# Wide exponents with the bias added by GpSimd, and low words of weights on ScalarE, in a Mamba-2 scan with an ELU layer

## The chip, the cores and the metric

The kernel runs on one core of a Trainium2 chip. The metric is the device time of one execution in microseconds (us); smaller is better. Five engines work from queues of their own, each strictly in its order: PE (TensorE, matrix products, with a separate weight load PEld), DVE (VectorE), ACT (ScalarE), POOL (GpSimd) and SP (SyncE, which here issues DMAs). PE writes to PSUM, a small memory that DVE and ACT read; the other tiles lie in SBUF.

## What is computed

The reference is a state-space scan (Mamba-2, in chunks) followed by a feed-forward layer with an ELU:

```python
# per batch b and head h, chunks c of 32 tokens (batch 4, heads 8, tokens 768, head_dim 32, state 16)
cum = np.cumsum(np.log(np.clip(a, 1e-6, 1.0)), axis=-1)        # within a chunk
L = np.exp(cum[:, :, :, None] - cum[:, :, None, :]) * causal   # "decay"
y_intra = einsum((C @ B.T) * L, x)
y_inter = einsum(C, state) * exp(cum)
state = decay_full * state + sum(B x * decay_from_j)
# then, on the 3072 tokens x 256 features
h = x @ w_in                                                   # 256 -> 2048
g = np.where(h > 0, h, np.exp(np.minimum(h, 0)) - 1)           # ELU
out = g @ w_out                                                # 2048 -> 256
```

The weights arrive as 64-bit floats. The kernel puts them together from their two 32-bit words itself.

## The kernel before

**Blocks.** The work is cut into twelve blocks `n` of 256 tokens (two halves `u` of 128; each half has two chunks `v` of 64 tokens, the chunk length that the kernel uses). Blocks two and three (`n` = 2 and 3) are those that the change touches.

**Decays.** For each block a tile `L` of 128 partitions x [8 heads, 2 halves, 64] is filled by a DMA that spreads the running sums along the partitions (`spread_cum`, L382). `decay_of(n, h)` (from L517) turns it into the decay of head `h` in place: two instructions on ACT (L521), each of 64 columns, take the exponent with a bias `ncum`, one column of [128, 1] for each half and head. After each fourth head, POOL sets what is not causal to zero with two `affine_select`s (L526), one for each chunk. `decay(n, q)` does heads 2q and 2q+1. `weigh(n, q)` (L550, DVE) then multiplies a PSUM tile of scores by two heads of `L`.

**Weight pieces.** There are 16 pieces of weights (0 to 7 are `w_in`, 8 to 15 `w_out`), each 128 x 512 numbers. For a piece `i`, `w_take` issues the absolute value of the high words on ACT (L196), the low words, and the signs on DVE (L223); `w_give` issues two DVE steps (L231, then L238) and the sum with the low words on POOL (L248). The low words are `x * 2**-51 + 2`. `w_low` can do them on DVE (L209) or on ACT (L205, with the bias from a column named `two`). Before the change, pieces 5 to 15 have them on DVE.

**The first layer, and the ELU.** `l1(n, i)` makes one product of the first layer, 8 matrix products (L666) into one PSUM tile, and appends it to a list `lag`. `elu()` takes the oldest: relu on ACT (L679), exponent on ACT (L686), and a combination on DVE (L688), which is the last reader of the PSUM tile. `l2(n, j)` adds to the second layer's sum (L826).

**PSUM.** Seven buffers hold all of these: products of `l1`, the four tiles of `scores` (L541), the state sums (`sums`, L571), the turned inputs (`turn`, L428, then L433 on ACT and L436 and L444 on DVE) and the four tiles of y (`across` L616, `inside` L634, copied out by ACT at L651). An eighth belongs to the second layer and some state sums. A product can only begin when a buffer has been read out.

**The order** is written out by hand: each engine's queue holds its instructions in the order in which the code issues them. Around the change there are two loops. The first has twelve steps `s`, each with one product `l1`; in its body stand, in this order, the decays of block two, `scores`, `sums` and the first two `weigh` of block two (step 7), a weight piece (`w_take`, `w_give`, in odd steps, pieces 5 to 10), `turn(2)` (step 5), the other `weigh` and `states(2)` (step 8), the first half of block three's decays (step 9), `across` and `inside` of block two (step 10), and at the end of the step the oldest `elu()` if more than one product waits:

```python
        if s < 8:
            decay_of(2, s)
        ...
        if s % 2 == 1 and todo < 11:
            w_take(todo, nc.vector)
            w_give(todo)
```

The second loop has eight steps `j`, with products of blocks two and three and pieces 11 to 15 (`j` = 0, 2, 3, 4, 5). Step 0 issues `turn(3)`, `w_give`, the waiting `elu()`s and then the second half of block three's decays; step 1 `scores(3)`, `sums(3)` and the four `weigh(3, q)`; step 2 `states(3)`; step 3 `inside(across(3), 3)`. Through `scan_ahead` it also takes the decays of blocks four and five, which the change does not touch, and from step 4 the preparation of a three-product form of the first layer (L735, L736, L754 to L771, L786) used for all later blocks, for which POOL subtracts parts of weights (L842).

Of the kernel before, what the change touches and what calls it, by code (L numbers as in the profile page):

```python
# [14 lines left out]
ALU = mybir.AluOpType  # L15
ACT = mybir.ActivationFunctionType

P = 128
Q = 64
# [13 lines left out]
def kernel(  # L33
# [27 lines left out]
    nc = tc.nc  # L61
    NB, NH, S, D = x.shape
    N = B.shape[-1]
    NG = S // BLK
# [27 lines left out]
    for k in range(4):  # L92
        (nc.scalar if k % 2 else nc.sync).dma_start(
            out=la0[BH * k:BH * (k + 1)],
            in_=a.rearrange("b h (c s) -> (b h) c s", s=P)[:, 0:2, :])
# [5 lines left out]
    st = {}  # L101

    def place(n):

        return 2 * (n // (2 * NG)) + n % 2, n // 2 % NG

    def rows_of(n):
        b, g = place(n)
        return slice(NG * NH * b + g, NG * NH * (b + 1), NG)
# [80 lines left out]
    def w_abs(i, cols=slice(None)):  # L190
        if i in (1, 2) or cols.start:
            w_abs_of[i, cols.start] = psum([P, 2, CW], "ps_mag").bitcast(U32)
        if i not in w_mag:
            w_mag[i] = (ffn.tile([P, 2, CW], U32, tag="tmp", name="mag", bufs=1) if i == 2 else
                        ffn.tile([P, 2, CW], U32, tag="g0", name="mag", bufs=12))
        nc.scalar.activation(  # L196
            w_abs_of.get((i, cols.start), w_mag[i])[:, :, cols].bitcast(F32),
            w_words(i)[1][:, :, cols].bitcast(F32), ACT.Abs)
# [4 lines left out]
    def w_low(i, eng, cols=slice(None)):  # L203
        if eng is nc.scalar:
            eng.activation(  # L205
                pieces[i][0][:, :, cols], w_words(i)[0][:, :, cols], ACT.Identity,
                scale=2.0 ** -51, bias=two)
        else:
            eng.tensor_scalar(  # L209
                out=pieces[i][0], in0=w_words(i)[0], scalar1=2.0 ** -51, scalar2=2.0,  # L210
                op0=ALU.mult, op1=ALU.add)
# [3 lines left out]
    def w_sign(i, cols=slice(None), eng=nc.vector):  # L215
        if i not in w_sgn:
            w_sgn[i] = ffn.tile([P, 2, CW], U32, tag="g1", name="sgn", bufs=12)
        if eng is nc.gpsimd:
            eng.tensor_scalar(
                out=w_sgn[i][:, :, cols], in0=w_words(i)[1][:, :, cols].bitcast(mybir.dt.int32),  # L220
                scalar1=0.0, scalar2=2.0 ** 31, op0=ALU.is_lt, op1=ALU.mult)
            return
        nc.vector.tensor_scalar(  # L223
            out=w_sgn[i][:, :, cols], in0=w_words(i)[1][:, :, cols], scalar1=0x80000000,
            scalar2=None, op0=ALU.bitwise_and)
# [53 lines left out]
    for v in range(2):  # L279
        nc.gpsimd.affine_select(  # L280
            out=low16[Q * v:Q * v + Q], in_=low16[Q * v:Q * v + Q], pattern=[[1, Q]],
            compare_op=ALU.is_ge, fill=-65536.0, base=0, channel_multiplier=-1)
# [4 lines left out]
        out=hmask, in_=hmask, pattern=[[-N, NH]], compare_op=ALU.is_ge, fill=0.0,  # L287
        base=0, channel_multiplier=1)
    nc.gpsimd.affine_select(
        out=hmask, in_=hmask, pattern=[[N, NH]], compare_op=ALU.is_ge, fill=0.0,  # L290
        base=N - 1, channel_multiplier=-1)
# [7 lines left out]
        out=minus, in0=ident, scalar1=-1.0, scalar2=None, op0=ALU.mult)  # L299


    heads = [first[:, 3, n].rearrange("p (h n) -> p h n", n=N) for n in range(2)]
# [57 lines left out]
    def turned(src, name, scale, eng):  # L360
        rows = src.shape[0]
        ps = psum([P, 2, rows], "ps_" + name)
        for u in range(2):
            nc.tensor.transpose(out=ps[:, u], in_=src[:, u], identity=ident[0:rows, 0:rows])
        t = const.tile([P, 2, rows], F32, name=name)
        if eng is nc.scalar:
            eng.copy(out=t, in_=ps)
        else:
            eng.tensor_scalar(out=t, in0=ps, scalar1=scale, scalar2=None, op0=ALU.mult)
        return t  # L370
# [142 lines left out]
    def decay(n, q):  # L513

        decay_of(n, 2 * q)
        decay_of(n, 2 * q + 1)

    def decay_of(n, h):
        L, row = st[n]["L"], rows_of(n).start + NG * h
        for u in range(2):  # L520
            nc.scalar.activation(  # L521
                L[:, h, u], L[:, h, u], ACT.Exp, bias=ncum[:, u, row:row + 1])
        if h % 4 == 3:
            for v in range(2):
                part = L[Q * v:Q * v + Q, h - 3:h + 1]
                nc.gpsimd.affine_select(  # L526
                    out=part, in_=part, pattern=[[0, 4], [0, 2], [1, Q]],
                    compare_op=ALU.is_ge, fill=0.0, base=0, channel_multiplier=-1)

# [15 lines left out]
    def weigh(n, q):  # L547
        s = st[n]
        M = att.tile([P, 2, 2, Q], F32, tag="M", name="M", bufs=8)
        nc.vector.tensor_tensor(  # L550
            out=M, in0=s["g"][q],
            in1=s["L"][:, 2 * q:2 * q + 2].rearrange("p k u i -> p u k i"), op=ALU.mult)
        s["M"].append(M)
# [104 lines left out]
    def l1(n, i, parts=1):  # L658

        ps = psum([P, 2, BLK], "ps_h")  # L660
        for j in range(2):
            m = 2 * i + j
            for part in range(parts):
                toks = slice(part * BLK // parts, (part + 1) * BLK // parts)
                for k in range(KC):
                    nc.tensor.matmul(  # L666
                        out=ps[:, j, toks], lhsT=w_in[i][:, k, j * P:(j + 1) * P],
                        rhs=yT[n // 2][:, k, n % 2].rearrange("p u i -> p (u i)")[:, toks],
                        start=(k == 0), stop=(k == KC - 1))
        lag.append((n, i, ps))  # L670
# [292 lines left out]
    def w_take(i, low):  # L963

        w_abs(i)
        w_low(i, low)
        w_sign(i)
# [15 lines left out]
    half = [slice(0, P), slice(P, 2 * P)]  # L983
# [97 lines left out]
    ncum = turned(F[:, 0], "ncum", -1.0, nc.vector)  # L1081
# [6 lines left out]
    todo = 5  # L1088
    for s, (n, i) in enumerate((
            (1, 0), (1, 1), (1, 2), (0, 4), (1, 3), (0, 5), (1, 4), (0, 6), (1, 5), (0, 7),  # L1090
            (1, 6), (1, 7))):
        l1(n, i, parts=2 if s < 2 else 1)
        if s < 8:
            decay_of(2, s)
        if s == 7:
            st[0] = kept
            scores(2)
            sums(2, 0, pool=p_o, tag="o", parts=(None, last))
            weigh(2, 0)
            weigh(2, 1)  # L1100
        if s % 2 == 1 and todo < 11:
            w_take(todo, nc.vector)
            w_give(todo)
            w_load(todo + 6)
            todo += 1
        if s in (1, 3):
            load_bc(3, us=(s // 2,))
        if s == 9:
            write_flat(0)
        if s == 4:  # L1110
            scaled(2, nc.gpsimd)
        if s == 5:
            turn(2)
            turn_exp(2)
        if s == 4:
            load_x(3)
            spread_exp(3)
        if s == 8:
            weigh(2, 2)
            weigh(2, 3)  # L1120
            states(0, last)
            st.pop(0)
            states(2)
        if s == 9:
            decay(3, 0)
            decay(3, 1)
        if s == 10:
            spread_cum(4)
            inside(across(2), 2)
        if len(lag) > 1:  # L1130
            elu()
# [38 lines left out]
    for j in range(2 * DIRECT):  # L1170
        n, i = 2 + j // DIRECT, j % DIRECT
        if j < 7:
            l2(0, j)
        piece = todo < len(pieces) and j != 1
        if j == 0:
            elu()
        if piece:
            w_take(todo, nc.vector)
        l1(n, i)
        if j == 7:  # L1180
            l2(0, j)
        if j == 0:
            scaled(3, nc.gpsimd)
            turn(3)
            elu()
            turn_exp(3)
        if piece:
            w_give(todo)
            todo += 1
        while lag:  # L1190
            elu()
        if j == 0:
            decay(3, 2)
            decay(3, 3)
        if j == 1:
            scores(3)
            sums(3)
            for q in range(4):
                weigh(3, q)
        if j == 2:  # L1200
            states(3)
        if j == 3:
            inside(across(3), 3)
        if j == 4:
            words_of_y(2)
        if j == 4:
            words_of_w(4)
        if j == 5:
            low_of_w(4)
        if j == 5:  # L1210
            both_of_y(2)
        scan_ahead(j)
        if j == 3:
            s_out[:] = weight_sums()
        if j == 6:
            differences(0, 4)
        if j == 7:
            words_of_w(5)
# [126 lines left out]
    n = NP - 2  # L1345
# [34 lines left out]
```

## Time and profile before

| | |
|---|---|
| median of 3 runs | 352.54 us (352.52 to 353.02) |
| span of the profiled execution, first to last instruction | 351.1 us |
| time of the profiled execution outside its span | not listed by itself; the median of the runs is 1.44 us above the span |
| TensorE clock granted | 1.000 |
| L521, exponents of 64 columns, all blocks | 160 instructions, 42.2 us, mean 337 ns |
| L526, masks on POOL | 40 instructions, 29.3 us, mean 733 ns |
| L209, low words on DVE | 11 instructions, 407 to 866 ns |
| L205, low words on ACT, 128x512 | 4 instructions, mean 753 ns |
| L248, sums of weight pieces on POOL, 128x512 | 15 instructions, mean 1276 to 1320 ns |
| L679 and L686, relu and exponent of the ELU, 128x512 | 24 each, mean 590 and 631 ns |

How to read it: the profile is that of one execution. A line such as L521 is a line of the kernel. A row of the timeline has the start in us, the duration in us, the engine, the line, the operation, the tile written and the tiles read, the shapes, and a count if instructions of one kind follow on each other; in brackets stand the idle time of that engine just before and what ended it. Consecutive instructions of one engine overlap a little, so that the next starts some 0.1 us before the row of the last one ends. A waits row names who waited for whom, and gives the total in us, the count and the longest one.

### The profile page before, as it was taken

To read this page: it belongs to the slowest core of one execution; us is meant where nothing else is said; L and a number is where in the kernel's file an instruction comes from. 1 tells how busy PE (TensorE), PEld (TensorE's weight loads), DVE (VectorE), ACT (ScalarE), POOL (GpSimd) and SP (SyncE) were. 2 spreads that over 40 slices of the span, in tenths; PEclk is the share of its full clock that TensorE was granted. 3 is DMA by queue.
4 is the path that set the end of the run, shared out by engine and by line. 5 is a ranking of instruction groups with operands and counts; after the bars stand their busy time and mean duration, and the time that the engine had idled before them with its cause. 6 is when DMAs were issued, how large, how long until landed. Compare 5 with 4: busy or idle time off the path is not lost.

```text
span 351.1 us, 9871 instructions
## 1 busy us (share of the span) xinstructions
PE 339.3 (97%) x3878; PEld 297.3 (85%) x3878; DVE 259.8 (74%) x515; ACT 234.8 (67%) x537; POOL 217.2 (62%) x338
## 2 busy tenths in 40 slices
PE   8789999998999999999999999999999999999995
PEld 5469888887777899988889988889988999999995
DVE  4798988879997899875878775878775766665332
ACT  5688989597748888657599447599457466565000
POOL 5563554566999599975196764196754164455760
PEclk9999999999999999999999999999999999999999
DMA  8887998370270421170421170320000100001002
GB/s 143 220 226 150 315 190 239 89 138 31 65 142 7 94 59 31 12 155 4 106 60 32 13 153 5 93 45 2 2 0 5 62 0 3 0 2 60 3 0 62
DMA packets 72727, 26.49 MB, mean 75 GB/s; under 512 B 57768, under 2 KB 67560, under 8 KB 72680
## 3 DMA queue, kind: packets, MB, share of 16 engines
q1 hardware_dynamic: 70360, 25.60, 31.7%
q8 instruction: 30, 0.49, 0.6%
q10 hardware_dynamic: 2320, 0.26, 0.5%
q14 instruction: 17, 0.14, 0.1%
HBM read 22.51 MB, written 3.34 MB: 74 GB/s over the span
## 4 chain that ended last, share of the span: by engine, by line
PE 82%; SPq 4%; DMA 4%; DVE 3%; POOL 3%; ACT 2%; issue 2%; POOLq 0%; DVEq 0%
PE ps_o L901 35%; PE ps_h L786 18%; PE ps_w L786 9%; PE ps_h L666 8%; PE ps_o L826 4%; PE ps_y L634 2%; DMA w<-in_moe_w_in_dram 2%; DMA xr<-in_x_dram 2%; PE ps_g L541 2%; SPq L178 2%; PE ps_y L616 1%; PE ps_st L571 1%; POOL L L526 1%; POOL w L842 1%; DVE y L761 1%
## 5 line engine op out<-in xcount | busy, mean ns | idle before, releaser
L901 PEld LDWEIGHTS ps_o<-w_out,g 128*128 128x128 f32 x640 | 78.5, 191 | 3.4
L901 PE MATMUL ps_o<-w_out,g 128*128 128x128 f32 x640 | 80.1, 275 | 0.0
L799 ACT ACTIVATE e<-ps_h 128x512 f32<-128x512 f32 x72 | 43.0, 597 | 46.8 <-DVE ps_h L793 46.8
L807 DVE SCALAR_TENSOR_TENSOR g<-e,ps_h 128x512 f32<-128x512 f32 x72 | 49.3, 685 | 32.4 <-ACT e L800 32.1
L842 POOL TENSOR_TENSOR g<-g 128x256 f32<-128x256 f32 x36 | 26.6, 739 | 58.1 <-DVE g L807 58.0
L793 DVE SCALAR_TENSOR_TENSOR ps_h<-ps_h,e 128x512 f32<-128x512 f32 x72 | 50.0, 695 | 12.0 <-ACT e L790 9.1
L790 ACT ACTIVATE e<-ps_w 128x512 f32<-128x512 f32 x72 | 42.3, 587 | 19.8 <-PE ps_w L786 19.7
L786 PE MATMUL ps_w<-y_both,w_words 128*128 128x512 f32 x144 | 52.0, 439 | 0.1
L666 PE MATMUL ps_h<-yT,w_in 128*128 128x256 f32 (+1 forms) x208 | 45.1, 367 | 3.5 <-POOL w_in L248 3.5
L800 ACT ACTIVATE e<-e 128x512 f32<-128x512 f32 x72 | 45.5, 632 | 2.3
L786 PE MATMUL ps_h<-y,w_words 128*128 128x512 f32 x144 | 45.6, 398 | 0.0
L786 PE MATMUL ps_h<-y,w 128*128 128x512 f32 x144 | 44.9, 392 | 0.2 <-POOL w L842 0.2
L666 PEld LDWEIGHTS ps_h<-yT,w_in 128*128 128x128 f32 x208 | 36.3, 190 | 9.4 <-POOL w_in L248 4.6
L521 ACT ACTIVATE L<-L,ncum 128x64 f32<-128x64 f32 x160 | 42.2, 337 | 0.2
L901 PE MATMUL ps_o<-w_sum,g 128*128 128x128 f32 x304 | 38.4, 275 | 0.0
L901 PEld LDWEIGHTS ps_o<-w_sum,g 128*128 128x128 f32 x304 | 37.0, 192 | 1.3 <-ACT e L790 0.2
L526 POOL TENSOR_SCALAR_AFFINE_SELECT L<-L 64x512 f32<-64x512 f32 x40 | 29.3, 733 | 9.6 <-ACT L L521 8.3
L786 PEld LDWEIGHTS ps_h<-y,w 128*128 128x128 f32 x144 | 27.0, 188 | 7.0 <-POOL w L842 0.7
L786 PEld LDWEIGHTS ps_h<-y,w_words 128*128 128x128 f32 x144 | 26.7, 188 | 6.2 <-issue 0.5
L842 POOL TENSOR_TENSOR g<-t,g 128x256 f32<-128x256 f32 x40 | 28.2, 736 | 5.8 <-PE ps_o L901 5.7
L826 PE MATMUL ps_o<-w_out,g 128*128 128x256 f32 x128 | 30.5, 382 | 1.0 <-POOL w_out L248 1.0
L842 POOL TENSOR_TENSOR g<-g,t 128x256 f32<-128x256 f32 x40 | 28.7, 753 | 0.2
(133 smaller groups left out, 536.7 us busy)
## 6 DMA issues: line engine op xcount, KB each, us to landing
L<-flat SPq DMA_DIRECT2D x20, 256.0 KB
w<-in_moe_w_out_dram SPq DMA_DIRECT2D x8, 512.0 KB
w<-in_moe_w_in_dram SPq DMA_DIRECT2D x7, 512.0 KB
xr<-in_x_dram SPq DMA_DIRECT2D x24, 128.0 KB
out_dram<-c_sum SPq DMA_DIRECT2D x9, 256.0 KB
bc<-in_B_dram SPq DMA_DIRECT2D x24, 64.0 KB
bc<-in_C_dram SPq DMA_DIRECT2D x22, 64.0 KB
ec<-flat_exp SPq DMA_DIRECT2D x10, 128.0 KB
```

What stands on the lines that cost most here:

```text
L521: nc.scalar.activation(L[:, h, u], L[:, h, u], ACT.Exp, bias=ncum[:, u, row:row + 1])
L526: nc.gpsimd.affine_select(out=part, in_=part, pattern=[[0, 4], [0, 2], [1, Q]], compare_op=ALU.is_ge, fill=0.0, base=0, channel_multiplier=-1)
L666: nc.tensor.matmul(out=ps[:, j, toks], lhsT=w_in[i][:, k, j * P:(j + 1) * P], rhs=yT[n // 2][:, k, n % 2].rearrange("p u i -> p (u i)")[:, ...
L786: nc.tensor.matmul(out=ps, lhsT=lhs[:, k], rhs=rhs[:, k], start=k == 0 and lhs is not w0, stop=k == KC - 1 and lhs is not w1)
L790: nc.scalar.activation(e, both, ACT.Copy, scale=WORD)
L793: nc.vector.scalar_tensor_tensor(out=high, in0=high, scalar=WORD - 1.0, in1=e, op0=ALU.mult, op1=ALU.add)
L799: nc.scalar.activation(e, high, ACT.Relu, scale=-1.0)
L800: nc.scalar.activation(e, e, ACT.Exp, scale=-1.0)
L807: nc.vector.scalar_tensor_tensor(out=g_of[n, m].rearrange("p b i -> p (b i)"), in0=e, scalar=1.0, in1=h, op0=ALU.subtract, op1=ALU.max)
L826: nc.tensor.matmul(out=o_of[n][:, ts], lhsT=g_of[n, j][:, m % 2, ts * P:(ts + 1) * P], rhs=w_out[:, m], start=(m == 0 and ts == 0), stop=( ...
L842: nc.gpsimd.tensor_tensor(out=out, in0=in0, in1=in1, op=ALU.subtract)
L901: nc.tensor.matmul(out=ps[:, ts], lhsT=b[:, ts * P:(ts + 1) * P], rhs=a[:, i], start=(i == chunk[0] and ts == 0), stop=(i == chunk[-1]), s ...
```

## The change

Block two's decays are no longer issued head by head in steps 0 to 7. Step 2 does heads 0 to 3 and step 4 heads 4 to 7 with a new function `decay_half`: one wide add on POOL of the bias (`ncum`, spread along 64 columns, 128 x 512 in all) onto half of the tile `L`, one wide exponent on ACT without a bias, and the two masks on POOL as before. Block three's halves do the same, at the places where its decays stood before (step 9 of the first loop, step 0 of the second). The low words of pieces 5 to 15 go from DVE to ACT. Nothing else is different; blocks four to eleven keep their decays.

```diff
+    def decay_half(n, half, eng=nc.gpsimd):
+
+        heads = slice(4 * half, 4 * half + 4)
+        part = st[n]["L"][:, heads]
+        rows = rows_of(n)
+        rows = slice(rows.start + 4 * NG * half, rows.start + 4 * NG * (half + 1), NG)
+        eng.tensor_tensor(
+            out=part, in0=part,
+            in1=ncum[:, :, rows].rearrange("p u h -> p h u").unsqueeze(3).to_broadcast(
+                [P, 4, 2, Q]), op=ALU.add)
+        nc.scalar.activation(part, part, ACT.Exp)
+        mask(n, half)
+
+    def mask(n, half):
+        for v in range(2):
+            part = st[n]["L"][Q * v:Q * v + Q, 4 * half:4 * half + 4]
+            nc.gpsimd.affine_select(
+                out=part, in_=part, pattern=[[0, 4], [0, 2], [1, Q]],
+                compare_op=ALU.is_ge, fill=0.0, base=0, channel_multiplier=-1)
+
     def decay_of(n, h):
         L, row = st[n]["L"], rows_of(n).start + NG * h
         for u in range(2):
             nc.scalar.activation(
                 L[:, h, u], L[:, h, u], ACT.Exp, bias=ncum[:, u, row:row + 1])
         if h % 4 == 3:
-            for v in range(2):
-                part = L[Q * v:Q * v + Q, h - 3:h + 1]
-                nc.gpsimd.affine_select(
-                    out=part, in_=part, pattern=[[0, 4], [0, 2], [1, Q]],
-                    compare_op=ALU.is_ge, fill=0.0, base=0, channel_multiplier=-1)
+            mask(n, h // 4)
...
         l1(n, i, parts=2 if s < 2 else 1)
-        if s < 8:
-            decay_of(2, s)
+        if s in (2, 4):
+            decay_half(2, s // 2 - 1)
...
         if s % 2 == 1 and todo < 11:
-            w_take(todo, nc.vector)
+            w_take(todo, nc.scalar)
             w_give(todo)
...
         if s == 9:
-            decay(3, 0)
-            decay(3, 1)
+            decay_half(3, 0)
...
         if piece:
-            w_take(todo, nc.vector)
+            w_take(todo, nc.scalar)
         l1(n, i)
...
         if j == 0:
-            decay(3, 2)
-            decay(3, 3)
+            decay_half(3, 1)
```

## The prediction

> **What bounds the kernel now.** I read the page first. TensorE is busy for 97% of the span, and the granted clock never leaves full speed.
>
> ```profile
> span 351.1 us, 9871 instructions
> PE 339.3 (97%) x3878; PEld 297.3 (85%) x3878; DVE 259.8 (74%) x515; ACT 234.8 (67%) x537; POOL 217.2 (62%) x338
> ```
>
> Next I cut the stretch that the change touches, 28 to 94 us, into windows. The columns are the stretch, its length, then busy time and instructions of each engine.
>
> ```profile
> core 0: us, PE busy (x) PEld busy (x) DVE busy (x) ACT busy (x) POOL busy (x), PEclk, DMA share, GB/s
> ...
> 28.00:34.00 6.00, 6.00 (x43) 5.63 (x44) 4.99 (x12) 5.76 (x15) 2.55 (x2) 1.00 0.87 171
> 34.00:40.00 6.00, 6.00 (x31) 5.30 (x30) 5.93 (x11) 5.40 (x13) 3.48 (x4) 1.00 0.95 318
> 40.00:46.00 6.00, 5.99 (x94) 4.84 (x94) 5.33 (x12) 5.87 (x14) 2.60 (x3) 1.00 1.03 246
> 46.00:52.00 6.00, 6.00 (x118) 5.00 (x118) 5.48 (x15) 4.85 (x18) 3.61 (x7) 1.00 0.95 186
> ...
> 82.00:88.00 6.00, 4.99 (x24) 4.28 (x24) 5.62 (x8) 3.45 (x11) 5.85 (x7) 1.00 0.14 47
> ```
>
> PE has no hole from 28 to 82, ACT and DVE are nearly full beside it, and POOL looks half free. The waits of PE from 24 to 100 us say how much a faster helper could give:
>
> ```profile
> PE ps_o L826 <- POOL w_out L248: 1.0, 1, 1.0
> PE ps_h L666 <- POOL w_in L248: 0.8, 1, 0.8
> PE ps_h L786 <- POOL w L842: 0.2, 1, 0.2
> ```
>
> The 0.8 lies at 23.4, ahead of the change. So the change can win some 1.2 us at most, at 82 and 92.7. What it can lose has no such bound: any wait that it puts between PE and its PSUM buffers adds to the end. So I walked the order of the queues, engine by engine.
>
> **Work removed and added.** 32 exponents of 64 columns leave ACT. In steps 0 to 7 of the list they cost 0.57 us per pair (32.03 to 32.60), and at 46.13 and 58.06 eight cost 2.0: 8.5 us in all. Four exponents of 512 columns come: L686 and L679, 512 wide without a bias column, take 0.59 to 0.63, so 2.5. Eleven low words come to ACT and leave DVE:
>
> ```profile
> L209 DVE TENSOR_SCALAR w_out<-w x8: 407/422/637, 44.2 to 79.8; 128x512 f32<-128x512 uint32 x8
> ...
> L205 ACT ACTIVATE w_in<-w,two x6: 516/744/769, 9.8 to 25.6; 128x512 f32<-128x512 uint32 x4, 128x256 f32<-128x256 uint32 x2
> ```
>
> That is 11 x 0.74 = 8.2 on ACT (0.65 from start to next start, 14.63 to 15.28). ACT's sum goes up by 2.2 us; DVE's falls by 0.33 each where it is backlogged. POOL gets four adds of 128x512: L248, also two inputs and 512 columns, takes 1.28 (1.52 at worst), and two of the broadcast products L408 (0.71 to 0.82 for 256 columns) 1.4 to 1.6. I take 1.3, nearest to L248. The masks only move with the decays; no DMA is moved or added.
>
> These sums would fit. What does not fit is the order. Each wide exponent now waits for an add on POOL, that add stands in POOL's queue behind the sum of the weight piece just given (L248), and that sum waits for DVE's high word (L238). Behind the waiting exponent stand ACT's relu and exponent of the next ELU, on which DVE's L688, PE's PSUM buffers and PE wait. Before, the exponents needed only data that lay ready, with the bias `ncum` there at 29.3.
>
> ```profile
> 31.47 0.69 DVE L238 SCALAR_TENSOR_TENSOR mag<-mag,sgn 128x512 uint32<-128x512 uint32 x1
> 32.03 0.57 ACT L521 ACTIVATE L<-L,ncum 128x64 f32<-128x64 f32 x2
> 32.24 1.27 POOL L248 TENSOR_TENSOR w_in<-mag,w_in 128x512 uint32<-128x512 uint32 x1 [1.79 <-DMA xr<-in_x_dram]
> ...
> 40.58 0.68 DVE L436 TENSOR_TENSOR ctm<-ps_tc,hmask 128x512 f32<-128x512 f32 x1
> ...
> 42.71 0.69 PE L541 MATMUL ps_g<-ctm,bct 32*64 32x128 f32 x32
> ...
> 50.31 1.66 ACT L651 COPY yT<-ps_y 128x128 f32<-128x128 f32 x6 [1.01 <-PE ps_y L634]
> 50.37 0.69 DVE L238 SCALAR_TENSOR_TENSOR mag<-mag,sgn 128x512 uint32<-128x512 uint32 x1
> 50.63 1.99 PE L666 MATMUL ps_h<-yT,w_in 128*128 128x256 f32 x8
> 51.14 1.26 POOL L248 TENSOR_TENSOR w_out<-mag,w_out 128x512 uint32<-128x512 uint32 x1 [2.04 <-DVE mag L238]
> ```
>
> In the working below, ELU on ACT is 1.15 from start to next start (L679 0.61, L686 0.54), an absolute value 0.58 (30.31 to 30.89), a low word 0.65.
>
> **First hole (block two).** DVE's L223, L231, L238 of piece 5 took 30.66 to 32.16 = 1.50; without L209 they follow at 30.08 and end 31.58. POOL's sum: 0.08 later, 1.28 long, 32.94. Add 1.3: 34.24; the exponent starts 34.29. ACT, from 29.12 with absolute value, low word and one ELU (2.38), is there at 31.50 and stands 2.8. Then exponent 0.54, ELU of step 1 to 35.98, absolute value of piece 6 done 36.65, low word and ELU of step 2 to 38.36. DVE: L231, L238 of piece 6 end 38.2 (L688 of step 1 at 36.1, then 0.60 and 1.50); sum 39.55, add 40.85, exponent 40.90: ACT stands 2.5 more. ELU of step 3 ends 42.7; L688 (0.60), 1.50 of piece 7, and ctm ends 45.4. It ended 41.26 before, 1.45 ahead of the scores; now the scores (42.71) wait for it. They and the state sums take five of seven PSUM buffers while two products hold the others, so the fifth is that of step 5's product: ACT's absolute value, low word, copy L433 (0.26) and two ELUs after 42.6 end 46.5, L688 at 47.2. The sums (43.34 to 44.00) then let the product of step 8 begin at 47.86 and not 44.00: **+3.9**.
>
> **Second hole (block three, first half).** DVE ran from L550 at 43.52 to the end of piece 9's L238 at 51.06 without a stop: 7.54, less two L209 of 0.33: 6.88. It now starts when the scores are there, 47.15: 54.03. Sum 55.37, add 56.67, exponent 56.72 (ACT, whose work ends 51.1, stands 5.6 us). Behind it: exponent 0.54, ELU of step 8 1.15, and only then the copies of block two's y (L651), 58.41. The first copy frees the buffer for step 11's product: 58.75, which began at 50.63 before. The shift is 8.1: **+4.2** here.
>
> **Third hole (second half).** ACT from 58.41: copies 1.68, four ELUs, two absolute values, two low words, one copy L433, so ELU (2,0) ends 67.5. DVE: L688 0.60, L444 0.34, L231 0.44, L238 0.69: 69.6; sum 70.9, add 72.2, exponent 72.3 to 72.8, ELU (2,1) to 74.1, L688 to 74.8. At that point six buffers belong to block three's scores and sums, whose readers (L550) follow this L688 on DVE, so product (2,2) begins at 74.8; before 62.81. The shift is 12.0: **+3.9**.
>
> **After that.** From j=2 on ACT waits for PE again (2.89 at 64.74, 0.68 at 68.19), so a low word fits, and all engines keep their distances to PE. At j=4 the low word delays ACT by 0.65 and with it L688 (74.81); DVE gets 0.33 back at j=5, ahead of the piece that PE waits for at 83.05. I take +0.3, between -1.2 (both waits gone) and +1.3 (two low words in full).
>
> Sum: 351.1 + 12.0 + 0.3 = 363.4 us of span. The median of the runs, 352.54, is 1.44 above the span shown; the page gives no other time of the profiled execution. So **364.8 us**.
>
> A row on the cover of DVE: the low word of piece 6 took 0.87 beside a mask on POOL (34.38), 0.42 elsewhere. [...]
>
> **Rivals.**
> - Less of it comes (0.15): one hole is covered, for instance because another PSUM buffer is free at (2,2). The buffers speak against it, since every candidate is released behind the same exponent. It gives 364.8 - 3.9 = 360.9; with two covered 357.
> - The clock drops in the holes (0.19). PE never stood over 1.69 us before, and the products after that hole (17.87) took 1.99, as those at 24.15 do, so the lower end is nothing. If PE ran at half pace for as long as it had stood, each hole of about 4 would add 2: one or two give 366.8 to 368.8, three 370.8. [...]
> - Faster (0.04): DVE's relief closes PE's waits at 83.05 and 92.68, 1.2 us, and 351.3 comes. It decides if the adds end before ACT reaches the exponents, at 31.5, 38.4 and 51.1. Against it: the adds would have to be 2.5 to 5.6 us earlier.
> - No change (0.02): both cancel, or slack that I missed swallows the holes.
> - My forecast has 0.60, from 362.5 to 367.
>
> The range 360.3 to 369.8 takes in the forecast, most of the clock case and the case with one hole covered; adds of 1.5 instead of 1.3 (four in the chains, +0.8) are inside. Faster by over 0.2% 0.04, within 0.2% 0.02 (the runs agree to about that, so less can't be told from no change), slower 0.94.
>
> **What would show it.** Right: ACT idle ahead of the exponents of the four wide decays, released by POOL, 2 to 6 us each; PE waiting ahead of L541 near 43, L666 near 55 and 71, about 4 us each; POOL adds near 1.3; no new hole after 80; fewer cuts in DVE. Wrong: adds that begin before the piece's sum on POOL, an exponent that does not hold the ELU behind it, or PE holes under 2 us.

## The result, and the profile after

The changed kernel takes 364.37 us (median of 5 runs, 363.75 to 365.17) where the kernel before takes 352.54 (5 runs, 351.65 to 353.02). The ratio is 1.0328, with a 95% interval of 1.031 to 1.0346, so it is slower by 3.3%. The profiled execution took 364.5 us, its span is 362.5, and its mean granted TensorE clock is 0.986.

Line numbers have moved. The new add is L524 and the wide exponent L528. Of the old lines L526 is now L534 (masks), L541 is L557 (scores), L550 is L566 (weigh), L571 is L587 (state sums), L651 is L667 (copies of y), L666 is L682 (first layer), L679, L686 and L688 are L695, L702 and L704 (ELU), L786 is L802, L826 is L842 and L842 is L858.

The first lines of the page after:

```profile
span 362.5 us, 9850 instructions
PE 345.7 (95%) x3878; PEld 301.7 (83%) x3878; DVE 252.9 (70%) x504; ACT 235.9 (65%) x520; POOL 220.6 (61%) x342
```

The sums of the helpers did what the change says: ACT stayed where it was (235.9 us, 234.8 before), DVE lost 6.9 us and POOL gained 3.4. Still, the span grew by 11.4, so the loss is not in the amount of work. PE's own busy time grew by 6.4 with as many instructions. The waits from 24 to 130 us show what is new; a row has who waited for whom, the total in us, the count and the longest one:

```profile
ACT L L528 <- POOL L L524: 15.1, 4, 5.5
...
PE ps_g L557 <- ACT e L695: 2.8, 1, 2.8
...
PE ps_h L682 <- ACT yT L667: 2.4, 1, 2.4
PE ps_h L682 <- DVE g L704: 2.2, 1, 2.2
...
PE ps_o L842 <- POOL w_out L248: 0.5, 1, 0.5
```

Each of the four wide exponents waited for its add, 15.1 us in all, and PE has three holes that were not there before. The wait for a piece of weights at block zero's last product of the second layer (1.0 before) is halved. The timeline of the first of the four waits shows how one comes about:

```profile
30.68 0.69 DVE L238 SCALAR_TENSOR_TENSOR mag<-mag,sgn 128x512 uint32<-128x512 uint32 x1
...
31.51 1.27 POOL L248 TENSOR_TENSOR w_in<-mag,w_in 128x512 uint32<-128x512 uint32 x1 [1.49 <-DVE mag L238]
...
32.74 1.06 POOL L524 TENSOR_TENSOR L<-L,ncum 128x512 f32<-128x512 f32 x1
...
33.83 0.63 ACT L528 ACTIVATE L<-L 128x512 f32<-128x512 f32 x1 [2.70 <-POOL L L524]
34.37 0.58 ACT L695 ACTIVATE e<-ps_h 128x512 f32<-128x512 f32 x1
```

Read it from below. The ELU's relu (L695) starts as soon as the exponent lets it, the exponent has stood 2.70 us for the add, the add begins when POOL has finished the sum of the weight piece, and POOL stood 1.49 us for DVE's step. The add and the exponent need nothing from that weight piece; only the order of the queues ties them together.

Windows of the same trace show the second effect, in the column PEclk (after the stretch and its length come busy time and instructions of PE, PEld, DVE, ACT and POOL, then the clock, the DMA share and GB/s):

```profile
46.00:52.00 6.00, 5.97 (x80) 4.83 (x81) 5.67 (x15) 4.44 (x8) 2.74 (x6) 0.72 0.99 223
...
58.00:64.00 6.00, 5.99 (x21) 5.10 (x22) 3.27 (x6) 5.82 (x13) 1.19 (x2) 0.75 0.28 74
...
76.00:82.00 6.00, 6.00 (x99) 4.85 (x102) 3.88 (x9) 4.18 (x10) 2.56 (x5) 0.83 0.88 171
```

Here PE is full, but it is granted 0.72, 0.75 and 0.83 of its clock. That is where most of its additional busy time comes from: after each hole it ran at half pace for a while (granted 0.50 for 3.41 us each time, last section), and the same products took 1.68, 1.46 and 1.83 us longer (worked out below), about 5.0 of the 6.4.

**Where the 11.4 us came from.** Take the same product in both traces. After the change the first loop's first product begins 0.44 us earlier (27.52 for 27.96), so 0.44 is added to the difference of each pair. Rows of the kernel before:

```profile
27.96 10.93 PE L666 MATMUL ps_h<-yT,w_in 128*128 128x128 f32 x64
...
44.00 5.45 PE L666 MATMUL ps_h<-yT,w_in 128*128 128x256 f32 x24
...
62.81 1.89 PE L666 MATMUL ps_h<-yT,w_in 128*128 128x256 f32 x8
```

Rows of the changed kernel (product (2,2) is shown further down):

```profile
27.52 10.93 PE L682 MATMUL ps_h<-yT,w_in 128*128 128x128 f32 x64
...
45.12 1.51 PE L557 MATMUL ps_g<-ctm,bct 32*64 32x128 f32 x32 [2.77 <-ACT e L695]
...
47.23 7.13 PE L682 MATMUL ps_h<-yT,w_in 128*128 128x256 f32 x24
...
58.01 3.45 PE L682 MATMUL ps_h<-yT,w_in 128*128 128x256 f32 x8 [2.41 <-ACT yT L667]
```


| product | before | after | shift |
|---|---|---|---|
| step 8, first product | 44.00 | 47.23 | +3.67 |
| step 11, first product | 50.63 | 58.01 | +7.82 |
| product (2,2) | 62.81 | 74.04 | +11.67 |
| `across` of block three | 68.08 | 81.10 | +13.46 |
| three-product form, first | 84.69 | 96.92 | +12.67 |
| last product, its end | 347.09 | 359.56 | +12.91 |

The last stores end 2.94 us after the last product, 4.01 before. So the span is 351.1 - 0.44 + 12.91 - 1.07 = 362.5.

### The profile page after: what moved, and what is told of

The parts are those of the page before. It is cut to its first block, busy times and chain, and to the rows that moved or that the text cites. A ratio compares the mean times of both kernels' runs of the same rounds, so it can differ in the third digit from the quotient of the medians.

```text
span 362.5 us, 9850 instructions
## 1 busy us (share of the span) xinstructions
PE 345.7 (95%) x3878; PEld 301.7 (83%) x3878; DVE 252.9 (70%) x504; ACT 235.9 (65%) x520; POOL 220.6 (61%) x342
## 4 chain that ended last, share of the span: by engine, by line
PE 71%; DVE 8%; ACT 7%; POOL 5%; issue 3%; SPq 2%; DMA 2%; POOLq 0%; DVEq 0%; ACTq 0%
PE ps_o L917 34%; PE ps_h L802 17%; PE ps_w L802 9%; PE ps_o L842 3%; PE ps_y L650 2%; PE ps_h L682 2%; DMA w<-in_moe_w_in_dram 2%; ACT e L702 2%; ACT e L695 2%; DVE g L704 2%; DVE mag L238 2%; PE ps_g L557 1%; PE ps_y L632 1%; POOL L L524 1%; POOL w_in L248 1%
## 5 line engine op out<-in xcount | busy, mean ns | idle before, releaser
L823 DVE SCALAR_TENSOR_TENSOR g<-e,ps_h 128x512 f32<-128x512 f32 x72 | 49.3, 685 | 32.0 <-ACT e L816 31.7
L858 POOL TENSOR_TENSOR g<-g 128x256 f32<-128x256 f32 x36 | 26.5, 736 | 58.4 <-DVE g L823 58.4
L682 PE MATMUL ps_h<-yT,w_in 128*128 128x256 f32 (+1 forms) x208 | 49.7, 393 | 6.7 <-ACT yT L667 2.4
L802 PE MATMUL ps_w<-y_both,w_words 128*128 128x512 f32 x144 | 51.5, 438 | 0.1
L682 PEld LDWEIGHTS ps_h<-yT,w_in 128*128 128x128 f32 x208 | 39.2, 205 | 14.0 <-POOL w_in L248 3.1
L802 PE MATMUL ps_h<-y,w_words 128*128 128x512 f32 x144 | 45.7, 398 | 0.0
L802 PE MATMUL ps_h<-y,w 128*128 128x512 f32 x144 | 45.0, 392 | 0.2 <-POOL w L858 0.2
L534 POOL TENSOR_SCALAR_AFFINE_SELECT L<-L 64x512 f32<-64x512 f32 x40 | 29.1, 729 | 12.4 <-ACT L L541 8.1
L541 ACT ACTIVATE L<-L,ncum 128x64 f32<-128x64 f32 x128 | 33.7, 336 | 0.0
L802 PEld LDWEIGHTS ps_h<-y,w 128*128 128x128 f32 x144 | 27.1, 188 | 7.0 <-POOL w L858 0.7
L704 DVE SCALAR_TENSOR_TENSOR g<-e,ps_h 128x512 f32<-128x512 f32 x24 | 16.4, 685 | 23.3 <-ACT e L702 23.3
L802 PEld LDWEIGHTS ps_h<-y,w_words 128*128 128x128 f32 x144 | 26.7, 188 | 6.2 <-issue 0.5
L858 POOL TENSOR_TENSOR g<-t,g 128x256 f32<-128x256 f32 x40 | 28.1, 734 | 5.8 <-PE ps_o L917 5.7
L842 PE MATMUL ps_o<-w_out,g 128*128 128x256 f32 x128 | 31.0, 388 | 0.5 <-POOL w_out L248 0.5
```

Of the source, the lines that this page charges most:

```text
L534: nc.gpsimd.affine_select(out=part, in_=part, pattern=[[0, 4], [0, 2], [1, Q]], compare_op=ALU.is_ge, fill=0.0, base=0, channel_multiplier=-1)
L541: nc.scalar.activation(L[:, h, u], L[:, h, u], ACT.Exp, bias=ncum[:, u, row:row + 1])
L682: nc.tensor.matmul(out=ps[:, j, toks], lhsT=w_in[i][:, k, j * P:(j + 1) * P], rhs=yT[n // 2][:, k, n % 2].rearrange("p u i -> p (u i)")[:, ...
L802: nc.tensor.matmul(out=ps, lhsT=lhs[:, k], rhs=rhs[:, k], start=k == 0 and lhs is not w0, stop=k == KC - 1 and lhs is not w1)
L823: nc.vector.scalar_tensor_tensor(out=g_of[n, m].rearrange("p b i -> p (b i)"), in0=e, scalar=1.0, in1=h, op0=ALU.subtract, op1=ALU.max)
L842: nc.tensor.matmul(out=o_of[n][:, ts], lhsT=g_of[n, j][:, m % 2, ts * P:(ts + 1) * P], rhs=w_out[:, m], start=(m == 0 and ts == 0), stop=( ...
```

## The experiments

The theory was the forecast's: what costs is the place of each add, behind a weight piece's sum on POOL, with the ELU behind the waiting exponent on ACT. Its rivals were that the low words cost ACT too much, that POOL is merely the wrong engine for the add, that the wide instructions themselves are slow, and that the granted clock makes the loss. The ratios are to the kernel before, run on the same chip.

**Low words alone on ScalarE.** The kernel before, with only the second part of the change.

```diff
-            w_take(todo, nc.vector)
+            w_take(todo, nc.scalar)
```

(in both loops.) Expected:

> Only the low words of pieces 5 to 15 go to ACT; all decays stay narrow, as before. Theory (order of the queues: the holes come from exponents that wait for POOL): no hole of 2 us, ACT merely gets 11 x 0.65 us longer; its ELUs run late by three low words at the state sums of block two (about +1.0), by two more at step 11's product and at product (2,2) (to +2.3), and by +0.3 after that: 355 us. Rival (ACT's extra work is the cause of the loss): most of the 12 us, 361 to 364 us.

Measured: 352.97 us, ratio 1.0018 (1.0003 to 1.0034). The loss that I expected was too large by 2 us. PE's wait at block zero's last product of the second layer fell from 1.0 to 0.3, but new waits came: 1.1 ahead of the state sums (to which the profile gives no cause), 0.3 for the copies of y, 0.3 for DVE's combination. The relief of DVE is real, and it is given back at once. As a cause of the 3.3% the low words are out.

**Decays alone.** The changed kernel with the low words back on DVE.

```diff
-            w_take(todo, nc.scalar)
+            w_take(todo, nc.vector)
```

> Only the decays of blocks two and three go wide, the low words stay on DVE. Theory: the three holes stay, since each chain (piece's high word, POOL's sum, POOL's add, exponent, ELU) is as long as in the full change, with L209 back in it and two low words less on ACT in the third: 362 to 364 us, ACT idle ahead of the four wide exponents for 2 to 6 us each. Rival (ACT's extra work): ACT is now 6 us lighter than before, so 352 to 353 us.

Measured: 366.01 us, 1.0395 (1.0372 to 1.0419), which is slower than the whole change and 2 us above the range that I expected. Its waits from 24 to 130 us:

```profile
ACT L L528 <- POOL L L524: 19.0, 4, 8.1
...
PE ps_g L557 <- DVE ctm L436: 3.7, 1, 3.7
...
PE ps_h L682 <- ACT yT L667: 2.7, 1, 2.7
...
PE ps_h L682 <- DVE g L704: 2.1, 1, 2.1
```

The exponents now wait 19.0 us, 3.9 more. The low words on DVE stand ahead of the step that POOL's sum needs, so each makes the chain longer. The two parts do not add up: alone they cost 0.6 and 13.6 us, together 11.8.

**The same work, adds issued earlier.** The whole change, but the add is split off and issued ahead of the weight piece: both adds of block two before the first loop, both of block three at step 6. Exponents and masks stay where the change has them.

```diff
-    def decay_half(n, half, eng=nc.gpsimd):
+    def bias_half(n, half, eng=nc.gpsimd):
...
+    def decay_half(n, half):
+        part = st[n]["L"][:, 4 * half:4 * half + 4]
         nc.scalar.activation(part, part, ACT.Exp)
         mask(n, half)
...
+    for h2 in range(2):
+        bias_half(2, h2)
...
+        if s == 6:
+            for h2 in range(2):
+                bias_half(3, h2)
```

> The full change, with the same instructions on the same engines, but POOL's adds are issued early: block two's two right after the bias is ready, ahead of the first loop, block three's two in step 6. Exponents and masks stay at their places. Theory (order): no exponent waits for POOL, the holes go, and DVE's relief takes half a microsecond off the wait before the last second-layer product of block zero: 351.5 to 352.7 us. Rival (the added work on POOL and ACT, 4 adds and 11 low words, is the cause): the same work stands in the same stretch, so 360 us or more.

Measured: 352.47 us, 1.0006 (0.9987 to 1.0026). All of the loss is gone with the same instructions, of the same sizes, on the same engines. This is the experiment that decides: the price was the place in the queue. No wait of an exponent for an add is left, and the granted clock is 1.000. PE's waits from 24 to 130 us:

```profile
PE ps_y L635 <- POOL Sx L612: 0.6, 1, 0.6
PE ps_h L685 <- DVE g L707: 0.3, 1, 0.3
PE ps_o L845 <- POOL w_out L248: 0.3, 1, 0.3
PE ps_y L635 <- DVE g L707: 0.2, 1, 0.2
PE ps_h L805 <- POOL w L861: 0.2, 1, 0.2
```

(Three lines lower than in the changed kernel: L635 is `across`, L685 the first layer, L845 the second.) There is no gain either. The timeline shows something that may have a part in it: the two adds of block three run beside DVE's steps of a weight piece.

```profile
43.49 2.26 POOL L524 TENSOR_TENSOR L<-L,ncum 128x512 f32<-128x512 f32 x2 [1.76 <-DMA L<-flat]
43.59 1.24 DVE L223 TENSOR_SCALAR sgn<-w 128x512 uint32<-128x512 uint32 x1
44.75 1.28 DVE L231 TENSOR_SCALAR mag<-mag 128x512 f32<-128x512 f32 x1
```

In the kernel before:

```profile
44.52 0.42 DVE L223 TENSOR_SCALAR sgn<-w 128x512 uint32<-128x512 uint32 x1
44.86 0.42 DVE L231 TENSOR_SCALAR mag<-mag 128x512 f32<-128x512 f32 x1
```

So L223 and L231 take 1.24 and 1.28 instead of 0.42, about as long as the adds beside them, and some 1.7 us of DVE are lost there. Block two's adds (29.82, 2.44 us for both) do the same to an L231 (1.28) and an L238 (1.43 instead of 0.69). That this is why nothing is won is not shown: the run with the adds placed apart, below, frees L223 and L231 of block three's adds and is no faster.

**Early adds without the low words.** The last kernel with the low words on DVE (the edit of the second experiment).

> As the run with early adds, but the low words stay on DVE: only the wide decays are left, with no exponent that waits for its add. Theory: the wide form by itself costs nothing when the order is right, 352.2 to 353.2 us; beside the run with decays alone (366.0) it takes away the whole loss with the same work on every engine. Rival (work of the adds on POOL): stays well above 355 us.

Measured: 353.69 us, 1.0028 (1.0004 to 1.0053), 0.5 us above the range that I expected. Against the decays alone at 366.01 this again takes nearly the whole loss away, so the low words were not what made the early adds work. The wait at block zero's last product of the second layer is back at 1.0.

**Only block two.** Block three gets its narrow decays back.

```diff
-            decay_half(3, 0)
+            decay(3, 0)
+            decay(3, 1)
...
-            decay_half(3, 1)
+            decay(3, 2)
+            decay(3, 3)
```

> The full change for block two, but block three keeps its sixteen narrow exponents at their old places; low words on ACT. Theory (three holes, each with its own wait): only the first hole is left, 3.7 us, and the products that ran slower after it (1.7) are no longer hidden by a second hole; some 0.5 us are lost to low words later: 357.5 to 358.5 us, with ACT waiting for POOL twice and not four times. If instead the waits share one cause that comes at once (a load too large for the stretch), the time stays above 362 us.

Measured: 357.27 us, 1.0132 (1.0103 to 1.016), 0.2 us below the range that I expected. Two exponents wait 4.9 us, PE has one hole of 2.8, and this costs 4.6 us. The change as a whole costs 11.8 - 4.6 = 7.2 more. That is not quite the price of the other two holes: here the slow products behind the first hole (24 took 7.01 us instead of 5.45) have no second hole to hide in. Counted as in the table above, the shift is +3.76 at step 8 and +5.32 at step 11.

**The add on DVE.** One word of the changed kernel.

```diff
-    def decay_half(n, half, eng=nc.gpsimd):
+    def decay_half(n, half, eng=nc.vector):
```

> The full change with the four wide adds on DVE instead of POOL, at the same places in the code. Theory (order: the exponent waits for the add and for what is queued ahead of the add): DVE does the add right behind the high word and not behind POOL's sum of the piece, so each exponent comes 1.3 us (the sum) plus 0.4 us (0.7 instead of 1.06 for the add) sooner, but still waits some 1.5 us in block two and more in block three; the shifts of PE would be some 1.5 at the scores, 3.7 at step 11, 5.6 at product (2,2): 357 to 360 us. [...]

Measured: 359.4 us, 1.0194 (1.0157 to 1.023). The add no longer stands behind POOL's sum, so the chain is shorter, but it stands in DVE's queue behind other work: three exponents wait 8.7 us for it, a fourth 2.2 (which the profile puts down to a DMA), and PE has two holes of 1.8. More than half of the loss (6.7 of 11.8 us) stays with another engine, so POOL as such is not the cause.

**Holes filled, to hold the clock.** The changed kernel with products that nobody reads in front of the holes: 6 of 128x512 ahead of block two's scores, 7 after its y, and 7 that add zeros to the second layer's sum ahead of product (2,2). `fill` (not shown) is `fill_new` with zeros as weights, into a sum that is already under way.

```diff
+    def fill_new(k):
+        ps = p_o.tile([P, 4, P], F32, tag="o", name="ps_fill")
+        for _ in range(k):
+            nc.tensor.matmul(
+                out=ps, lhsT=ident, rhs=ident.unsqueeze(1).to_broadcast([P, 4, P]),
+                start=True, stop=True)
...
+            fill_new(6)
...
+            fill_new(7)
...
+        if j == 2:
+            fill(7, o_of[0].rearrange("p t e -> p (t e)"))
```

> The full change, with PE kept busy in the three holes: 6, 7 and 7 products of 128x512, whose results are not used or add zeros. Theory (order): the waits of ACT stay as they are and the holes only close over; the granted clock stays at 1.00, which gains what the slow products after the third hole cost, 1.34 for L682 and 0.49 for L842, as the slow ones after the first two are hidden behind the next hole: 362.5 us. Rival (the dropped clock is the main loss): all slow products count, 1.7 + 1.6 + 1.8, and the time falls below 360 us.

Measured: 368.63 us, 1.0463 (1.0445 to 1.048). This one is inconclusive: a product took some 0.9 us, so the fills lasted 5.3 to 6.3 us, longer than the holes, and pushed the end out by themselves. The clock did stay at 1.00. So I repeated it with half of them (3, 4 and 4):

> As the run with filled holes, but with 3, 4 and 4 filling products of 0.87 us, so that they end before each hole does (2.6, 3.5, 3.5 us). Theory: the waits of ACT stay, the granted clock stays at 1.00, and the gain is what the slow products after the third hole cost: 362 to 363 us. Rival (the dropped clock is a main loss): below 360 us. If the clock costs nothing, 364.4 us.

Measured: 363.06 us, 1.0296 (1.0268 to 1.0324). The clock is 1.000, and the four waits of ACT are still 15.1 us. Against the change as it stands that is 1.3 us less in the medians; the two intervals (1.0268 to 1.0324 and 1.031 to 1.0346) overlap a little, so the size is rough. The products behind the third hole show where it is. With the clock held:

```profile
74.31 1.99 PE L698 MATMUL ps_h<-yT,w_in 128*128 128x256 f32 x8 [0.20 <-DVE g L720]
76.14 1.89 PE L858 MATMUL ps_o<-w_out,g 128*128 128x256 f32 x8
```

In the changed kernel:

```profile
74.04 3.23 PE L682 MATMUL ps_h<-yT,w_in 128*128 128x256 f32 x8 [2.23 <-DVE g L704]
77.06 2.38 PE L842 MATMUL ps_o<-w_out,g 128*128 128x256 f32 x8
```

The same 16 products end at 78.03 with the fills and at 79.44 without, 1.4 us later, or 1.7 if each trace is counted from the first loop's first product (27.78 with the fills, 27.52 without). So the clock is a small part, 1.3 to 1.8 us of 11.8, and the waits that make the holes come without it.

**Adds placed apart.** To win what the early adds lost to DVE, block three's adds were moved: the first to the end of step 8, with its exponent and masks in step 11, the second also to step 11.

```diff
-        if s == 6:
-            for h2 in range(2):
-                bias_half(3, h2)
...
             states(2)
+            bias_half(3, 0)
-        if s == 9:
+        if s == 11:
             decay_half(3, 0)
+            bias_half(3, 1)
```

> As the run with early adds, but block three's adds come apart: the first at the end of step 8, behind the state products on POOL, with its exponent and masks in step 11 (ahead of them the copies of y), the second in step 11, with its exponent in step 0 of the second loop as before. The run with early adds lost 0.3, 0.2 and 0.6 us in new small waits after DVE's L223 and L231 took 1.24 and 1.28 us instead of 0.42 beside those two adds; here no add lies ahead of the state products: those waits go, the wait ahead of block zero's last second-layer product stays at 0.3 instead of 1.0, and the time is 351.4 to 352.2 us, just below before. If it is not, DVE's relief of 11 low words buys nothing at all.

Measured: 352.53 us, 1.0003 (0.9986 to 1.0021). I expected a gain, and none can be told. DVE stood 1.53 us for a mask on POOL (L537 at 62.26, which itself stood behind the sum of a weight piece), and PE still waited 0.6 for POOL's `Sx`, four instructions that took 1.97 us there and 1.42 before. Neither comes from the new place of the adds: the run with early adds has the same 1.53 (at 65.12), 0.6 and 1.97, and in the kernel before DVE stood 0.82 for that mask (63.53). In all three the masks stand behind the sum of piece 11.

**Masks placed as well.** The second add goes to step 9, after that step's weight piece, and its exponent and masks ahead of piece 11 in step 0 of the second loop.

```diff
+        if s == 9:
+            bias_half(3, 1)
         if s == 11:
             decay_half(3, 0)
-            bias_half(3, 1)
...
         if j == 0:
             elu()
+            decay_half(3, 1)
         if piece:
             w_take(todo, nc.scalar)
...
-        if j == 0:
-            decay_half(3, 1)
```

> As the run with placed adds, but block three's second half comes sooner: its add in step 9 (behind piece 9's sum on POOL), its exponent and masks in step 0 of the second loop ahead of piece 11 and not behind it. In the run with placed adds DVE stood 1.53 us for those masks and the state products of block three came 0.6 us too late for PE. Theory: that wait goes, and PE is left with 0.3 and 0.2 us: 351.7 to 352.3 us, a ratio of 0.997 to 0.999. If the time stays at 352.5, the relief of DVE has nothing left to give in this stretch.

Measured: 352.32 us against 353.14, ratio 0.9982 (0.9964 to 1.0). This is the best version, about 0.2% below the kernel before and at the very edge of what can be told from no change. The wait for `Sx` is gone. What PE waits for from 24 to 130 us (the 0.8 for `w_in` lies ahead of the change; "issue" means that the profile shows nothing that PE waited for):

```profile
PE ps_h L685 <- POOL w_in L248: 0.8, 1, 0.8
PE ps_st L590 <- issue: 0.8, 1, 0.8
PE ps_y L653 <- issue: 0.7, 1, 0.7
PE ps_o L845 <- POOL w_out L248: 0.5, 1, 0.5
PE ps_h L805 <- POOL w L861: 0.2, 1, 0.2
```

The forecast's bound holds: some 1.2 us could be won at block zero's last product of the second layer and at the three-product form, and of the 1.0 at the former half is left here. The 0.8 ahead of the state sums (L590, at 61.06) is new. By the times it ends when DVE's combination of an ELU (60.27 to 60.96) has read out a PSUM buffer, and that combination had stood 1.57 us for ACT; this was not tested.

## Why the prediction was right, point by point

**The bound** was right. PE was full from 28 to 82 us, and no version won more than 0.2%, while the order of the queues lost up to 4.0% (the decays alone).

**The waits of ACT** were right in place, cause and size. Forecast 2.8, 2.5, 5.6 and 4.8 us (from 67.5 to 72.3), measured 2.70, 2.23, 5.53 and 4.64, all released by the add. Early adds took them away, and the loss with them.

**The add's duration** was too high: 1.3 assumed from L248, 1.05 to 1.06 measured. Four adds lie in the chains, so by the working this is worth 4 x 0.24, some 1.0 us; the shift at product (2,2) shows 0.33 of it, and what took up the rest is open.

**The shifts** were right: forecast +3.9, +8.1 and +12.0, measured +3.67, +7.82 and +11.67, lower by 0.2 to 0.3. Block two alone supports the first (+3.76 at step 8).

**"About 4 us each" for PE's waits was wrong**; they were 2.77, 2.41 and 2.23. The shift is set by the chain through DVE, POOL and ACT, and PE's share of it is partly waiting and partly slower work. In the first hole the scores took 1.51 us from first to last instead of 0.69: after the first six the weight load stood 0.34 us (the profile names DVE's combination, which reads out a buffer, as what ended it), and what took the rest of the 0.82 is not shown. 2.77 + 0.82 = 3.6. Before the second hole 24 instructions of the first layer took 7.13 us instead of 5.45, at half pace up to 50.75: 2.41 + 1.68 = 4.1. Before the third, eight took 3.45 instead of 1.99: 2.23 + 1.46 = 3.7. Those sums are, to within 0.2, the steps between the shifts: 3.67, 4.15 and 3.85. So the drops of the clock behind the first two holes cost nothing in this change: PE was early for the next hole anyway, and only waited less there. Where no further hole follows, as with block two alone, the first drop does count (7.01 us for 5.45).

**The clock** was a rival with 0.19, at 366.8 to 370.8. A drop came three times, its price once: behind the third hole no other hole follows, and 3.23 + 2.38 us for what takes 1.89 + 1.89 gives +1.83. The next row of the table, +13.46, is 11.67 and this. The forecast's sum had nothing for it. I had priced the rival as if each drop went to the end, and at half pace for as long as PE had stood. No run shows that length, which was my assumption: the changed kernel shows 0.50 for 3.41 us with each of the waits of 2.77, 2.41 and 2.23.

**The rest of the way** was set at +0.3 and was -0.8 up to the three-product form (13.46 to 12.67), of which 0.5 is the wait at block zero's last product of the second layer, halved; then +0.24 came back up to the end, and the stores ended 1.07 sooner. Terms that were mis-sized in both directions met: the span was forecast at 363.4 and is 362.5, while the median lies 1.87 above the span instead of 1.44.

**DVE's steps beside POOL's** lost little in this change. L223 took 0.67 or 0.68 instead of 0.42 twice (29.64 beside a sum of a weight piece, 42.63 beside L408), and no new add ran beside L223 or L231. More was lost with the early adds, where L223 and L231 took 1.24 and 1.28 beside two adds. The forecast's 0.42 "elsewhere" for a low word was read too narrowly: in the kernel before L209 also took 0.60 to 0.66 at 30.08, 38.23, 56.82 and 70.82, each time beside a sum of a weight piece on POOL. Beside a wide add the DVE step lasted about as long as the add (2.26 us for the two) and lost 0.82 to 0.86, nearly twice the 0.45 of the forecast's row (0.87 for 0.42). What slows it no trace shows.

## What to carry to other kernels

When a step is split over two engines, its first half stands in the other engine's queue behind whatever was issued there before, and the engine that waits for it takes its whole queue along (here four exponents stood 15.1 us for their adds, and PE 7.4 us in three holes): look at what stands ahead of the producer and behind the consumer, before adding up durations. If the producer's inputs lie ready, issue it earlier, at a place where its engine is idle and where it does not run beside a step that it slows (here DVE's L223 and L231, from 0.42 to some 1.25 us). A bottleneck that is full has little to win and much to lose by a change beside it, and part of what a hole costs can show as slower work and not as waiting (here 2.77 us of waiting in a shift of 3.67), so take the shift from the chain that sets the end, and not from the sum of the waits.

## What the runs showed of the hardware that was not expected

**The clock dropped to 0.50 around waits of 2.2 to 2.8 us**, where the forecast's rival reckoned with holes of about 4. The granted clock was 0.50 from 47.34 to 50.75, from 57.58 to 60.99 and from 74.64 to 78.05 in the changed kernel. These times are worked out from the means of windows of half a us, such as

```profile
47.00:47.50 0.50, 0.50 (x25) 0.41 (x9) 0.50 (x3) 0.47 (x1) 0.00 (x0) 0.84 1.46 144
...
50.50:51.00 0.50, 0.50 (x4) 0.39 (x3) 0.43 (x3) 0.00 (x1) 0.47 (x2) 0.75 0.51 123
```

with 0.50 in all windows between: 0.84 is 0.16 us at half pace, up to 47.50, and 0.75 is 0.25 us, from 50.50. Each stretch is 3.41 us long, and their starts are 10.24 and 17.06 us apart, three and five times 3.41. The holes that go with them were waits of 2.77, 2.41 and 2.23 us; with the add on DVE one of 1.85 was followed by some 7 us at half pace, one of 1.81 by none, and one of 1.69 in the kernel before by none. The first drop began 2.2 us after PE had resumed (45.12), the second 0.4 before (58.01), the third 0.6 after (74.04). How long PE must stand for a drop, and what else it takes, stays open.

**The add with a broadcast operand was no slower than the sum of a weight piece.** The wide add on POOL, with one column spread over 64, took 1.05 to 1.06 us for 128x512 where it ran alone, and the sum of a weight piece, of the same size without a spread operand but on integers, 1.27. The two differ in type as well, so what the spread operand by itself costs is open.
